# A second DRAM layout for the running sums of log a, and decays of half the first group read from it

## Chip, cores, metric

One NeuronCore of a Trainium2 chip runs the whole program. The metric is the device time of one execution in microseconds; lower is better. Before the change three runs gave 578.08, 579.09 and 579.59 us, a median of 579.09 us.

## What is computed

A decaying linear attention (chunked state-space form) is followed by two mixture-style feed-forward layers. The reference, cut to what matters:

```python
# batch 4, heads 8, seq 768, head_dim 32, d_state 16, chunks of 32
cum = np.cumsum(log_a_chunk, axis=-1)
L = np.exp(cum[..., :, None] - cum[..., None, :]) * causal      # decay from j to i
M = einsum('bhin,bhjn->bhij', Cc, Bc) * L
y = einsum('bhij,bhjd->bhid', M, xc) + einsum('bhin,bhnd->bhid', Cc, state) * exp(cum)[..., None]
state = exp(sum(log_a_chunk)) * state + sum_j Bx * exp(cum_last - cum)
# then, on [3072, 256]:
h = max(x @ w1, x @ w2, x @ w3) @ w_out                         # d_ff 768
z = h @ w_in                                                    # d_ff 2048
out = ((a0 + a1 z + a2 z^2 + a3 z^3) / (1 + |b0||z| + |b1| z^2 + 1e-6)) @ w_out2
```

## The kernel before

The kernel takes chunks of 128 time steps, so that there are six groups (g = 0 to 5) of all four batches, and splits a group into eight units (one batch, four heads). **Stage one** is the attention, some 100 us; **stage two** is the two feed-forward layers, group by group, with fp32 weights split in a high and a low part and three matmuls per product.

Per unit of stage one: `d_mm` (L482) forms the exponent of the decay, cum_i - cum_j below the diagonal and -4096 above, in a PSUM bank `d` on TensorE; ScalarE takes its exponential `e` (L504); `s_mm` (L468) gives the products of C and B, two units at a time; VectorE multiplies the two to `m` (L509); `y_intra` (L511) multiplies `m` with x. Once a group, `state` (L549 to L573) brings the state forward, `y_inter` adds its part, and `prep` (L451) decays C and B by `e0` and `wrev`.

There are two ways to the exponent. In the first group (g = 0) VectorE multiplies the triangle with log a (`tl`, L494) and an fp32 matmul sums that (L490). In the later groups it is one bf16 matmul of two operands in the tiles `lr0` and `lr1`, which serve the groups in turn: constant rows of ones (the input `lrc`) and rows of the running sums, in three bf16 parts that add up to fp32. Those sums are made once: `cum_mm` (L399), split into three parts `cs` on ScalarE and VectorE, one write to DRAM as `cum_d` with the part outermost (L417), and then, for each group from 1 on, `load_cum` (L424) reads them back in seven loads: one for the row operand `rd`, three for `ld`, three for `re`, the operand of the matmul that spreads the decay of C (`sel`, a small matrix of ones copied from lr, L436).

The weights come as 64-bit values in 28 pieces of 512 KB (`plan_conv`, L213): a transfer to one of three raw buffers `wraw` (L241), two passes on ScalarE (L246, L249), three on VectorE (L247, L250, L253), two halves each of two passes on GpSimd (L258, L262), and a copy on ScalarE in between. The names w1, w2, w3 come three times each, then wo (3), win (8), and for stage two wo2 (8).

All transfers are issued by SyncE, in one order. The order on every engine is made ahead by a planner (`Plan.emit`, L91): it takes operations with a cost and a due time and lists them; each engine then runs its list strictly in order. Transfers whose name stands in the list `FIRST` (L37) are due before everything else.

Of the kernel before, what the change touches and what calls it, by code (L numbers as in the profile page):

```python
# [19 lines left out]
CH = 128  # L20
# [10 lines left out]

OL = 6
# [4 lines left out]
FIRST = ["a", "t", "b0", "z0", "n0", "x0", "w1"]  # L37
# [119 lines left out]
def decay_attention_max_moe_rational_moe(  # L157
# [119 lines left out]
    def mark():  # L277
        return _Tile(lambda: None)
# [40 lines left out]
    for nm, bufs in (("pd", 2), ("psc", 4), ("py", 2)):  # L319
# [15 lines left out]
    sel = sp.tile([24, 128], BF16, name="sel")  # L335
# [3 lines left out]
    (act_t, tri_t, trib_t, own_t, la_t, wrev_t, cs_t, sel_t, cum_t, co_t) = (mark() for _ in range(10))  # L339
    rd_t, ld_t, re_t = ([mark() for _ in range(2)], [[mark() for _ in range(3)] for _ in range(2)],  # L340
                        [[mark() for _ in range(3)] for _ in range(2)])
# [75 lines left out]
    load(lambda: cum_d.rearrange("p q r i -> r (p q) i"), cs.rearrange("r p q i -> r (p q) i"), [cum_t], [cs_t], kb=295)  # L417

    for i in (1, 0):
        op("dve", 0.5, lambda i=i: dve.memset(lr[i][64:128].bitcast(F32), 0.0), [], [lr_t[i]])  # L420
        load(lambda i=i: lr[i][0:64], lrc, [lr_t[i]], kb=197, nm=f"l{i}")
    load(lambda: co_raw, coef, [co_t, own_t], kb=68)

    def load_cum(g):  # L424
        q, i, j = g // 3, g % 2, g % 3
        load(lambda: rd[i][0:24], cum_d[:, q].rearrange("p (g u f) i -> p g u (f i)", u=NU, g=3)[:, j],
             [rd_t[i]], [cum_t, lr_t[i]], kb=25)
        for p in range(3):
            load(lambda p=p: ld[i][24 + 4 * p:28 + 4 * p],
                 cum_d[p, q].rearrange("(g u f) j -> g f u j", u=NU, g=3)[j], [ld_t[i][p]], [cum_t, lr_t[i]], kb=16)  # L430
        for p in range(3):
            load(lambda p=p: re[i][8 * p:8 * p + 8].rearrange("h (b i) -> h b i", b=NB),
                 cum_d[p, q].rearrange("(g b h) i -> g h b i", b=NB, g=3)[j], [re_t[i][p]], [cum_t], kb=16)


    op("dve", 0.2, lambda: dve.tensor_copy(  # L436
        out=sel.rearrange("r (q n f) -> r q n f", q=2, f=4),
        in_=ld[1][0:24, :, 0].rearrange("r (q f) -> r q f", q=2)[:, :, None, :].to_broadcast([24, 2, NS, 4])),
       [lr_t[1]], [sel_t])
# [42 lines left out]
    def d_mm(u):  # L482
# [8 lines left out]
        if g == 0:  # L491
# [104 lines left out]
    prep(0)  # L596
    load_cum(1)
# [307 lines left out]
def layout(inputs):  # L905
# [62 lines left out]
```

## Time and profile before

| | |
|---|---|
| median of three runs | 579.09 us |
| the profiled execution, own time | 579.21 us |
| its span (first to last instruction) | 577.3 us |
| TensorE busy | 556.8 us, 96% |
| VectorE, ScalarE, GpSimd busy | 89%, 75%, 76% |
| mean granted TensorE clock | 0.997 |
| read from DRAM, written | 27.27 MB, 5.91 MB |

The profile is one execution. Its page gives the busy share of every engine; the other views used below are the timeline of one engine, the busy time of all engines in chosen windows, the chain of work that ended last, and the instructions of one tensor. PE is TensorE, DVE VectorE, ACT ScalarE, POOL GpSimd, SPq the queue of SyncE that issues transfers. A bracket at the end of a timeline row tells how long the engine stood idle before it and what released it.

### The profile page before, as it was taken

The numbers are of one execution on the slowest core, as the hardware profiler recorded it, in microseconds if no ns is written. First come the engines' busy times: TensorE is split into PE (matmuls) and PEld (weight loads), VectorE is DVE, ScalarE is ACT, GpSimd is POOL, SyncE is SP. The second block draws the span as 40 slices with busy tenths as digits, with TensorE's granted clock in tenths as the row PEclk, the third lists the DMA queues.
The fourth block names the chain that finished last, engine by engine and source line by source line (L and its number), as shares of the span: only waits on it lengthen the run. The fifth ranks groups of instructions, "written<-read, shape, count | busy, mean of one in ns | idle before, by whom it ended". The sixth has DMA issues, their size and how long they took to land.

```text
span 577.3 us, 8164 instructions
## 1 busy us (share of the span) xinstructions
PE 556.8 (96%) x2747; PEld 411.2 (71%) x2758; DVE 511.9 (89%) x777; ACT 435.3 (75%) x756; POOL 440.6 (76%) x410
## 2 busy tenths in 40 slices
PE   8989989989999999999999999999999999999997
PEld 3333433768787788888888888888888888886563
DVE  7888979777999999998889988898898889988996
ACT  4677768556888878878788787778777877778883
POOL 1756767887989967778677877687777997869883
PEclk9999999999999999999999999999999999999999
DMA  6877864533000000101000010000000010000000
GB/s 216 243 270 238 237 233 148 182 110 109 1 1 2 18 20 0 37 1 38 0 1 37 1 33 6 0 20 18 1 1 1 0 37 0 1 1 36 2 0 36
DMA packets 19047, 33.71 MB, mean 58 GB/s; under 512 B 3526, under 2 KB 4030, under 8 KB 19006
## 3 DMA queue, kind: packets, MB, share of 16 engines
q1 hardware_dynamic: 19003, 33.20, 17.9%
q8 instruction: 21, 0.34, 0.2%
q14 instruction: 23, 0.16, 0.1%
HBM read 27.27 MB, written 5.91 MB: 57 GB/s over the span
## 4 chain that ended last, share of the span: by engine, by line
PE 53%; DVE 17%; POOL 17%; issue 4%; ACT 4%; DMA 3%; SPq 2%; POOLq 0%; ACTq 0%; DVEq 0%
PE pg L650 7%; PE pg L652 7%; PE pg L651 6%; PE ph L650 5%; PE ph L652 5%; PE ph L651 5%; PE po L652 4%; PE po L650 4%; PE po L651 4%; POOL glo L853 2%; PE s L477 2%; DMA wraw<-in_w_dram 2%; POOL v L819 2%; POOL hlo L295 2%; DVE pr L845 2%
## 5 line engine op out<-in xcount | busy, mean ns | idle before, releaser
L853 POOL TENSOR_TENSOR glo<-w,ghi 128x512 fp32r<-128x512 f32 x80 | 105.5, 1319 | 16.2 <-ACT ghi L196 16.1
L650 PE MATMUL pg<-xhi,w_hi 128*128 128x512 f32 x202 | 79.1, 392 | 2.8 <-DVE xa L732 2.2
L652 PE MATMUL pg<-xhi,w_lo 128*128 128x512 f32 x202 | 78.8, 390 | 0.0
L651 PE MATMUL pg<-xlo,w_hi 128*128 128x512 f32 x202 | 78.7, 390 | 0.0
L840 ACT ACTIVATE pr<-v,qc 128x512 f32<-128x512 f32 x83 | 57.4, 693 | 22.2 <-DVE v L826 11.3
L295 POOL TENSOR_TENSOR hlo<-xa,hhi 128x512 fp32r<-128x512 f32 x36 | 49.5, 1376 | 26.0 <-ACT hhi L196 25.9
L258 POOL TENSOR_TENSOR wa<-wa,we 128x256 uint32<-128x256 uint32 x56 | 44.2, 800 | 32.9 <-DVE wa L253 32.9
L196 ACT ACTIVATE ghi<-w 128x512 fp32r<-128x512 f32 x80 | 50.4, 630 | 23.9 <-PE po L652 14.2
L650 PE MATMUL ph<-yhi,win_hi 128*128 128x512 f32 x160 | 62.7, 392 | 1.7 <-DVE w L838 1.5
L651 PE MATMUL po<-glo,wo_hi 128*128 128x512 f32 x160 | 62.4, 390 | 0.4 <-POOL glo L853 0.4
L652 PE MATMUL ph<-yhi,win_lo 128*128 128x512 f32 x160 | 62.3, 390 | 0.0
L650 PE MATMUL po<-ghi,wo_hi 128*128 128x512 f32 x160 | 62.3, 390 | 0.0
L652 PE MATMUL po<-ghi,wo_lo 128*128 128x512 f32 x160 | 62.3, 390 | 0.0
L651 PE MATMUL ph<-ylo,win_hi 128*128 128x512 f32 x160 | 62.3, 389 | 0.0
L845 DVE SCALAR_TENSOR_TENSOR pr<-w,co,pr 128x512 f32<-128x512 f32 x83 | 61.9, 746 | 0.0
L819 POOL TENSOR_TENSOR v<-t,v 128x512 f32<-128x512 f32 x44 | 58.1, 1320 | 2.8
L842 DVE SCALAR_TENSOR_TENSOR v<-v,pr 128x512 f32<-128x512 f32 x83 | 56.2, 677 | 2.2 <-ACT pr L841 2.2
L847 DVE SCALAR_TENSOR_TENSOR w<-v,pr 128x512 f32<-128x512 f32 x83 | 56.3, 678 | 0.4
L841 ACT ACTIVATE pr<-pr 128x512 f32<-128x512 f32 x86 | 50.5, 587 | 0.9
L732 DVE TENSOR_TENSOR xa<-xa,pg 128x512 f32<-128x512 f32 x67 | 45.5, 679 | 2.3 <-PE pg L652 2.1
L650 PEld LDWEIGHTS pg<-xhi,w_hi 128*128 128x128 f32 x202 | 37.9, 188 | 12.1 <-DVE xa L732 3.1
L837 POOL TENSOR_TENSOR w<-w,t 128x512 f32<-128x512 f32 x20 | 25.9, 1293 | 24.0 <-DVE v L826 22.1
(167 smaller groups left out, 1485.1 us busy)
## 6 DMA issues: line engine op xcount, KB each, us to landing
wraw<-in_wo_dram SPq DMA_DIRECT2D x11, 512.0 KB
wraw<-in_w_dram SPq DMA_DIRECT2D x9, 512.0 KB
wraw<-in_win_dram SPq DMA_DIRECT2D x8, 512.0 KB
xn<-in_xn_dram SPq DMA_DIRECT2D x6, 512.0 KB
out_dram<-ob SPq DMA_DIRECT2D x12, 256.0 KB
xt_d<-xo SPq DMA_DIRECT2D x10, 256.0 KB
xst<-xt_d SPq DMA_DIRECT2D x10, 256.0 KB
bt<-in_bz_dram SPq DMA_DIRECT2D x6, 256.0 KB
```

What stands on the lines that cost most here:

```text
L196: act.activation(out=o, in_=i, func=AF.Copy)
L295: lambda: e.tensor_tensor(out=lo.t, in0=src(), in1=hi.t.bitcast(F32), op=ALU.subtract),
L650: pe.matmul(dst, wh, hi, start=first, stop=False)
L651: pe.matmul(dst, wh, lo, start=False, stop=False)
L652: pe.matmul(dst, wl, hi, start=False, stop=last)
L819: pop(1.23, lambda: pool.tensor_tensor(out=f(v), in0=f(t1), in1=f(v), op=ALU.mult), [t1], [v])
L840: aop(0.62, lambda: act.activation(out=f(r), in_=f(v), func=AF.Ln, bias=qc), [v], [r])
L841: aop(0.48, lambda: act.activation(out=f(r), in_=f(r), func=AF.Exp, scale=-1.0), [], [r])
L842: dop(0.61, lambda: dve.scalar_tensor_tensor(out=f(v), in0=f(v), scalar=QC, in1=f(r), op0=ALU.add, op1=ALU.mult), [r], [v])
L845: dop(0.61, lambda: dve.scalar_tensor_tensor(out=f(r), in0=f(w), scalar=c(0), in1=f(r), op0=ALU.add, op1=ALU.mult), [w], [r])
L847: dop(0.61, lambda: dve.scalar_tensor_tensor(out=f(w), in0=f(v), scalar=2.0, in1=f(r), op0=ALU.subtract, op1=ALU.mult), [v, r], [w])
L853: pop(1.23, lambda: pool.tensor_tensor(out=f(lo), in0=f(w), in1=f(hi).bitcast(F32), op=ALU.subtract), [w, hi], [lo])
```

## The change

The sums are written to DRAM a second time, as `cup_d`, with the part next to the row, in two writes (one for groups 0 to 2, one for 3 to 5). From this layout one load brings all three parts for `ld` and one all three for `re`, so a group takes three loads. The rows of `lrc` are put in the new order. Group 0 loads its `rd` and `ld` as well (named `r0` in `FIRST`), and its units 4 to 7 take the bf16 way; units 0 to 3 keep `tl`. `lrc` carries the matrix `sel` in 128 more columns, so the copy on VectorE goes; the memsets of `lr` go from VectorE to GpSimd; `lr0` is loaded early (`l0` in `FIRST`).

```diff
+ND = 4
-FIRST = ["a", "t", "b0", "z0", "n0", "x0", "w1"]
+FIRST = ["a", "t", "b0", "z0", "l0", "n0", "x0", "w1", "r0"]
...
     cum_d = dram.tile([3, 2, 96, CH], BF16, name="cum_d")
+    cup_d = dram.tile([2, 96, 3, CH], BF16, name="cup_d")
...
-    lr = [sp.tile([128, NU * CH + T], BF16, name=f"lr{i}") for i in range(2)]
+    lr = [sp.tile([128, NU * CH + T + 128], BF16, name=f"lr{i}") for i in range(2)]
...
-    sel = sp.tile([24, 128], BF16, name="sel")
+    sel = lr[1][0:24, NU * CH + T:]
...
     load(lambda: cum_d.rearrange("p q r i -> r (p q) i"), cs.rearrange("r p q i -> r (p q) i"), [cum_t], [cs_t], kb=295)
-    for i in (1, 0):
-        op("dve", 0.5, lambda i=i: dve.memset(lr[i][64:128].bitcast(F32), 0.0), [], [lr_t[i]])
-        load(lambda i=i: lr[i][0:64], lrc, [lr_t[i]], kb=197, nm=f"l{i}")
+    for q in range(2):
+        load(lambda q=q: cup_d[q], lambda q=q: cs[:, :, q], [cup_t], [cs_t], kb=148)
+    for i in (0, 1):
+        op("pool", 0.9, lambda i=i: pool.memset(lr[i][64:128].bitcast(F32), 0.0), [], [lr_t[i]])
+        load(lambda i=i: lr[i][0:64], lrc, [lr_t[i]], kb=213, nm=f"l{i}")
...
     def load_cum(g):
         q, i, j = g // 3, g % 2, g % 3
+        nm = None if g else "r0"
         load(lambda: rd[i][0:24], cum_d[:, q].rearrange("p (g u f) i -> p g u (f i)", u=NU, g=3)[:, j],
-             [rd_t[i]], [cum_t, lr_t[i]], kb=25)
-        for p in range(3):
-            load(lambda p=p: ld[i][24 + 4 * p:28 + 4 * p],
-                 cum_d[p, q].rearrange("(g u f) j -> g f u j", u=NU, g=3)[j], [ld_t[i][p]], [cum_t, lr_t[i]], kb=16)
-        for p in range(3):
-            load(lambda p=p: re[i][8 * p:8 * p + 8].rearrange("h (b i) -> h b i", b=NB),
-                 cum_d[p, q].rearrange("(g b h) i -> g h b i", b=NB, g=3)[j], [re_t[i][p]], [cum_t], kb=16)
+             [rd_t[i]], [cum_t, lr_t[i]], kb=25, nm=nm)
+        rows = cup_d[q].rearrange("(g r) p i -> g r p i", g=3)[j]
+        load(lambda: ld[i][24:36], rows.rearrange("(u f) p j -> f p u j", u=NU),
+             [ld_t[i]], [cup_t, lr_t[i]], kb=49, nm=nm)
+        if g:
+            load(lambda: re[i].rearrange("r (b i) -> r b i", b=NB), rows.rearrange("(b h) p i -> h p b i", b=NB),
+                 [re_t[i]], [cup_t], kb=49)
...
-    op("dve", 0.2, lambda: dve.tensor_copy(
-        out=sel.rearrange("r (q n f) -> r q n f", q=2, f=4),
...
-        if g == 0:
+        if u < ND:
...
     prep(0)
+    load_cum(0)
     load_cum(1)
...
-            lrc[24 + 4 * p + f, NU * CH + CH * f:NU * CH + CH * f + CH] = -1.0
+            lrc[24 + 3 * f + p, NU * CH + CH * f:NU * CH + CH * f + CH] = -1.0
```

The planner sorts everything anew. Line numbers of the changed kernel are two to six higher. Three places show what that moved.

**SyncE, from the load of the constant rows `lrc` on.** Names: `lr1`, `lr0`, `re1` are the tiles above, `cz1` is C of a group, `wraw_...` a raw weight piece, `DMAHW0` to `DMAHW7` the eight counters on which transfers report in turn. Before:

```order
L283 DMA lr1_126<-in_lrc_dram 64x1536 [waits DMAHW6_49]
L283 DMA bt_232<-in_bz_dram 128x512 [waits DMAHW7_49]
L283 DMA cz1_135<-in_ct_dram 32x512 [waits DMAHW0_49,Pool_49]
L283 DMA re1_128<-cum_d_83 8x4x128 [waits DMAHW3_49,DMAHW1_49]
L283 DMA re1_128<-cum_d_83 8x4x128 [waits DMAHW2_49]
L283 DMA re1_128<-cum_d_83 8x4x128
L241 DMA wraw_255<-in_w1_dram 128x2x512 [waits DMAHW4_49,DVE_49,Activation_49]
L283 DMA cz1_135<-in_ct_dram 32x512 [waits DMAHW5_49]
L283 DMA cz1_135<-in_ct_dram 32x512 [waits DMAHW6_49]
L283 DMA cz1_135<-in_ct_dram 32x512 [waits DMAHW7_49]
L283 DMA xn_284<-in_xn_dram 128x1024 [waits DMAHW0_49]
L283 DMA lr1_126<-cum_d_83 24x1x512 [waits DMAHW1_49]
```

And now, from the second write of `cup_d` (the 19th transfer) to the load of `lr0` from it (the 30th):

```order
L287 DMA cup_d_84<-cs_133 288x1x128 [waits DMAHW2_49]
L287 DMA lr0_126<-cum_d_83 24x1x512 [waits DMAHW5_49,DMAHW3_49]
L287 DMA cz1_135<-in_ct_dram 32x512 [waits DMAHW4_49,Pool_49]
L245 DMA wraw_262<-in_w1_dram 128x2x512 [waits DVE_49,Activation_49]
L287 DMA cz1_135<-in_ct_dram 32x512 [waits DMAHW6_49]
L287 DMA cz1_135<-in_ct_dram 32x512 [waits DMAHW7_49]
L287 DMA cz1_135<-in_ct_dram 32x512 [waits DMAHW0_49]
L287 DMA xn_294<-in_xn_dram 128x1024 [waits DMAHW1_49]
L287 DMA bn_297<-in_bn_dram 128x512 [waits DMAHW2_49]
L287 DMA lr1_127<-cum_d_83 24x1x512 [waits DMAHW3_49]
L245 DMA wraw_304<-in_w2_dram 128x2x512 [waits DMAHW4_49,DVE_49,Activation_49]
L287 DMA lr0_126<-cup_d_84 12x8x128 [waits DMAHW5_49]
```

The first group's sums stand where group 1's stood, behind the second pieces of w1 and w2; the three early loads of `re1` have gone from ahead of the second w1 piece.

**TensorE, around the fifth unit's exponent.** `d_...` are the exponents, `s_...` the products of C and B, `y_...` the outputs. Before, the fifth unit (`d_246`) stood before the first `y`:

```order
L488 LDWEIGHTS trib_124
L488 MATMUL d_246<-trib_124 128x512
L490 MATMUL d_246<-tl_238,tri_s_123 128x512
L520 MATMUL y_262<-m_224,xn_171 32x128 x4
L520 MATMUL y_268<-m_250,xn_171 32x128 x4
```

And now (`d_343`), behind the products of C and B for all eight units and the outputs of the first four:

```order
L479 MATMUL s_266<-cz0_134,bt_143 128x512
L479 MATMUL s_267<-cz0_134,bt_143 128x512
L522 MATMUL y_240<-m_264,xn_172 32x128 x4
L522 MATMUL y_257<-m_274,xn_172 32x128 x4
L479 MATMUL s_290<-cz0_134,bt_143 128x512
L479 MATMUL s_291<-cz0_134,bt_143 128x512
L490 LDWEIGHTS trib_125
L490 MATMUL d_343<-trib_125 128x512
L492 LDWEIGHTS lr0_126
L492 MATMUL d_343<-lr0_126 128x512
```

Between the last `s` and the first row on `lr0` only the constant part of the exponent stands.

**VectorE, up to the fifth unit's product** (`m_367` before, `m_360` now; the rows on `wa` are weight conversions, three to a piece). Before:

```order
L494 TENSOR_TENSOR tl_306<-tri_s_123,la_130 128x512
L253 SCALAR_TENSOR_TENSOR wa_257<-wraw_214,wa_257 128x512
L509 TENSOR_TENSOR m_330<-s_229,e_252 128x512
L247 TENSOR_SCALAR wa_314<-wa_314 128x512
L566 TENSOR_TENSOR st_344<-d_319,co_raw_84 128x512
L250 TENSOR_SCALAR wa_314<-wa_314 128x512
L436 COPY sel_133<-lr1_126 24x128
L253 SCALAR_TENSOR_TENSOR wa_314<-wraw_220,wa_314 128x512
L509 TENSOR_TENSOR m_367<-s_290,e_297 128x512
```

And now:

```order
L511 TENSOR_TENSOR m_274<-s_250,e_246 128x512
L251 TENSOR_SCALAR wa_271<-wa_271 128x512
L254 TENSOR_SCALAR wa_271<-wa_271 128x512
L257 SCALAR_TENSOR_TENSOR wa_271<-wraw_221,wa_271 128x512
L251 TENSOR_SCALAR wa_312<-wa_312 128x512
L254 TENSOR_SCALAR wa_312<-wa_312 128x512
L257 SCALAR_TENSOR_TENSOR wa_312<-wraw_225,wa_312 128x512
L464 TENSOR_TENSOR bn_297<-bn_297,wrev_132 128x512
L251 TENSOR_SCALAR wa_331<-wa_331 128x512
L254 TENSOR_SCALAR wa_331<-wa_331 128x512
L257 SCALAR_TENSOR_TENSOR wa_331<-wraw_262,wa_331 128x512
L511 TENSOR_TENSOR m_360<-s_266,e_353 128x512
```

Four pieces of weights are converted before the fifth product where three were, and the second `bn` is decayed before it.

## Rows read from the trace of the kernel before

**Rows 1.** The page, part 1: busy us (share) and instructions of each engine.

```profile
PE 556.8 (96%) x2747; PEld 411.2 (71%) x2758; DVE 511.9 (89%) x777; ACT 435.3 (75%) x756; POOL 440.6 (76%) x410
```

**Rows 2.** Windows: length, busy us by engine, granted clock (PEclk), DMA share, GB/s.

```profile
14.30:23.40 9.10, 9.10 (x69) 3.70 (x67) 9.10 (x17) 6.94 (x12) 6.22 (x8) 1.00 0.84 244
23.40:32.40 9.00, 6.64 (x52) 2.12 (x51) 5.67 (x9) 5.71 (x11) 5.25 (x6) 1.00 0.94 269
...
60.00:100.00 40.00, 34.67 (x341) 14.69 (x345) 35.54 (x61) 30.03 (x54) 28.36 (x37) 1.00 0.65 206
100.00:126.00 26.00, 23.20 (x105) 18.16 (x106) 20.44 (x26) 15.25 (x28) 22.50 (x26) 1.00 0.43 145
126.00:131.00 5.00, 5.00 (x16) 3.92 (x16) 3.02 (x6) 2.89 (x6) 2.89 (x3) 0.66 0.28 105
131.00:570.00 439.00, 436.46 (x1873) 349.94 (x1872) 399.69 (x593) 346.00 (x597) 353.22 (x304) 1.00 0.04 14
```

**Rows 3.** Timeline, TensorE: start, us, line, out<-in; fifth unit's matmul, first one on lr.

```profile
14.49 1.02 PE L490 MATMUL d<-tl,tri_s 128*128 128x512 f32 x2
...
24.12 0.38 PE L490 MATMUL d<-lr 128*128 128x512 bf16 x1
```

**Rows 4.** Timeline, VectorE, three windows; in brackets the idle time before and its releaser.

```profile
14.84 2.06 DVE L494 TENSOR_TENSOR tl<-tri_s,la 128x512 f32<-128x512 f32 x2
...
22.69 2.47 DVE L509 TENSOR_TENSOR m<-s,e 128x512 f32<-128x512 f32 x4
...
30.70 0.69 DVE L462 TENSOR_TENSOR bn<-bn,wrev 128x512 f32<-128x512 f32 x1 [3.33 <-DMA bn<-in_bn_dram]
...
81.25 0.43 DVE L247 TENSOR_SCALAR wa<-wa 128x512 f32<-128x512 f32 x1 [3.23 <-ACT wa L246]
...
99.27 0.68 DVE L509 TENSOR_TENSOR m<-s,e 128x512 f32<-128x512 f32 x1
```

**Rows 5.** Timeline, GpSimd, 0 to 40 us.

```profile
0.73 1.84 POOL L368 MEMSET cz<- 128x1024 f32 x2 [0.29 <-POOLq L953]
...
14.47 1.88 POOL L258 TENSOR_TENSOR wa<-wa,we 128x256 uint32<-128x256 uint32 x2 [11.90 <-DVE wa L253]
```

**Rows 6.** One tensor's instructions, cum_d: issue in ns, minimum/median/maximum.

```profile
L283 SPq DMA_DIRECT2D lr<-cum_d x20: 286/393/817, 19.7 to 69.2; - x20
```

**Rows 7.** Timeline, SyncE's queue, 0 to 60 us: start and length of each issue.

```profile
9.85 0.34 SPq L283 DMA_DIRECT2D cum_d<-cs  x1
...
13.30 1.15 SPq L283 DMA_DIRECT2D re<-cum_d  x3
...
14.81 0.40 SPq L241 DMA_DIRECT2D wraw<-in_w_dram  x1
...
19.70 2.00 SPq L283 DMA_DIRECT2D lr<-cum_d  x4
...
22.69 0.38 SPq L241 DMA_DIRECT2D wraw<-in_w_dram  x1
```

**Rows 8.** The chain that ended last, 0 to 130 us: weight pieces under way (start, us).

```profile
5.70 5.33 DMA wraw<-in_w_dram
...
22.69 6.27 DMA wraw<-in_w_dram
...
73.72 6.16 DMA wraw<-in_win_dram
```

**Rows 9.** Timeline, ScalarE, 0 to 40 us.

```profile
28.98 0.66 ACT L249 ACTIVATE we<-wraw 128x512 uint32<-128x512 uint32 x1 [2.71 <-DMA wraw<-in_w_dram]
...
29.55 1.07 ACT L504 ACTIVATE e<-d 128x512 f32<-128x512 f32 x2
```

**Rows 10.** Timeline, TensorE, 123 to 136 us.

```profile
125.80 0.50 PE L650 MATMUL pg<-xhi,w_hi 128*128 128x512 f32 x1 [1.94 <-DVE xa L732]
...
127.82 0.63 PE L651 MATMUL ph<-xlo,w_hi 128*128 128x512 f32 x1
128.24 0.63 PE L652 MATMUL ph<-xhi,w_lo 128*128 128x512 f32 x1
```

More of the change, by code (lines that the diff above doesn't have):

```diff
@@ L323, in decay_attention_max_moe_rational_moe @@
     trib = sp.tile([128, 2, 128], BF16, name="trib")
-    lr = [sp.tile([128, NU * CH + T], BF16, name=f"lr{i}") for i in range(2)]
+    lr = [sp.tile([128, NU * CH + T + 128], BF16, name=f"lr{i}") for i in range(2)]
     ld = [t[:, 0:NU * CH].rearrange("p (u j) -> p u j", u=NU) for t in lr]
-    rd = [t[:, NU * CH:] for t in lr]
+    rd = [t[:, NU * CH:NU * CH + T] for t in lr]
     re = [sp.tile([24, T], BF16, name=f"re{i}") for i in range(2)]
@@ L334, in decay_attention_max_moe_rational_moe @@
     cs = sp.tile([96, 3, 2, CH], BF16, name="cs")
-    sel = sp.tile([24, 128], BF16, name="sel")
+    sel = lr[1][0:24, NU * CH + T:]
     cz = [sp.tile([128, 4, T], F32, name=f"cz{i}") for i in range(2)]
     cz_t, lr_t = [[mark() for _ in range(4)] for _ in range(2)], [mark() for _ in range(2)]
-    (act_t, tri_t, trib_t, own_t, la_t, wrev_t, cs_t, sel_t, cum_t, co_t) = (mark() for _ in range(10))
-    rd_t, ld_t, re_t = ([mark() for _ in range(2)], [[mark() for _ in range(3)] for _ in range(2)],
-                        [[mark() for _ in range(3)] for _ in range(2)])
+    (act_t, tri_t, trib_t, own_t, la_t, wrev_t, cs_t, cum_t, cup_t, co_t) = (mark() for _ in range(10))
+    rd_t, ld_t, re_t = ([mark() for _ in range(2)] for _ in range(3))
     xg, bg, ctg, btg = {}, {}, {}, {}
@@ L425, in load_cum @@
         q, i, j = g // 3, g % 2, g % 3
+        nm = None if g else "r0"
         load(lambda: rd[i][0:24], cum_d[:, q].rearrange("p (g u f) i -> p g u (f i)", u=NU, g=3)[:, j],
-             [rd_t[i]], [cum_t, lr_t[i]], kb=25)
-        for p in range(3):
-            load(lambda p=p: ld[i][24 + 4 * p:28 + 4 * p],
-                 cum_d[p, q].rearrange("(g u f) j -> g f u j", u=NU, g=3)[j], [ld_t[i][p]], [cum_t, lr_t[i]], kb=16)
-        for p in range(3):
-            load(lambda p=p: re[i][8 * p:8 * p + 8].rearrange("h (b i) -> h b i", b=NB),
-                 cum_d[p, q].rearrange("(g b h) i -> g h b i", b=NB, g=3)[j], [re_t[i][p]], [cum_t], kb=16)
-    op("dve", 0.2, lambda: dve.tensor_copy(
-        out=sel.rearrange("r (q n f) -> r q n f", q=2, f=4),
-        in_=ld[1][0:24, :, 0].rearrange("r (q f) -> r q f", q=2)[:, :, None, :].to_broadcast([24, 2, NS, 4])),
-       [lr_t[1]], [sel_t])
+             [rd_t[i]], [cum_t, lr_t[i]], kb=25, nm=nm)
[5 more added lines that the diff above has]
+                 [re_t[i]], [cup_t], kb=49)
     op("act", 0.2, lambda: act.activation(out=co[:, 4:6], in_=co_raw[:, 4:6], func=AF.Abs), [co_t], [co_t])
@@ L455, in prep @@
             op("pe", 0.22, lambda: pe.matmul(p0.t, sel, re[g % 2], start=True, stop=True),
-               [sel_t, *re_t[g % 2]], [p0], when["p0", g])
+               [lr_t[1], re_t[g % 2]], [p0], when["p0", g])
             e0[g] = new("s2", "e0", 2)
@@ L501, in d_mm @@
             op("pe", 0.46, lambda: mm(lambda: ld[g % 2][:, k], lambda: rd[g % 2]),
-               [trib_t, lr_t[g % 2], rd_t[g % 2], *ld_t[g % 2]], [t], when["d", u])
+               [trib_t, lr_t[g % 2], rd_t[g % 2], ld_t[g % 2]], [t], when["d", u])
         e_t[u] = e = new("s4", "e", 4)
@@ L931, in layout @@
     d["tri"] = tri.astype(np.float32)
-    lrc = np.zeros((64, NU * CH + T), np.float32)
+    lrc = np.zeros((64, NU * CH + T + 128), np.float32)
     for p in range(3):
+        for h in range(NH):
+            lrc[3 * h + p, NU * CH + T + 64 * (h // 4) + h % 4:NU * CH + T + 64 * (h // 4) + 64:4] = 1.0
         for u in range(NU):
```

## The prediction

> **What bounds the kernel now.** The page first: TensorE is busy for nearly the whole span [rows 1]. The windows by stage then show where it isn't [rows 2]: from 131 to 570 us it has 436.46 of 439 us, so stage two has no room in it, and only its start can move. The room lies in stage one, up to about 100 us, and in the first group of stage two up to 131 us: TensorE stands for 2.4 us in 23.4 to 32.4 us, for 5.3 in 60 to 100, for 2.8 in 100 to 126, and runs at a lower clock from 126 to 131. In 60 to 100 us VectorE has 35.54 of 40 us, as much as TensorE, so in stage one VectorE's order sets the pace as often as TensorE's. The DMA share is 0.84 and 0.94 in the two stretches from 14.3 to 32.4 us: there the transfers queue up, and a small one waits behind big ones. That queue is what this change gets into.
>
> **TensorE and VectorE work removed.** For units 4 to 7 of the first group the fp32 matmul on tl, 1.02 us, becomes a bf16 one on lr, 0.38 us [rows 3]: 4 x 0.64 = 2.6 us less on TensorE. VectorE loses four products tl (two took 2.06 us [rows 4]), 4.1 us, the two memsets of lr and the copy to sel. Both savings lie before the point where, below, both engines stand and wait for a load, so I cost them at nothing; what they free is used or lost in that wait. The memsets go to GpSimd, which made two larger ones in 1.84 us and then stood for 11.90 us [rows 5]: two of 0.1 to 0.92 us fit in there, cost nothing.
>
> **SyncE's queue.** A group's sums came in seven loads and now in three: 35 loads in all become 17 (five groups by three, and two for the first group), against two more writes. Loads to lr took 0.39 us in the median [rows 6], so SyncE spends some 16 x 0.39 = 6 us less on issuing. It is on the path only where a weight piece stands behind such loads. I take 1.0 us for this, between nothing and the 3.2 us that VectorE waited at 81.25 us [rows 4] behind a weight piece that was 6.16 us under way [rows 8].
>
> **The new wait.** The fifth unit's matmul started at 14.49 us, on data made on the chip [rows 3]. Now it needs the first group's sums from DRAM. SyncE issues in order, and the order shown above has the load of lr0 from cup_d as the 30th transfer, behind two weight pieces, xn, bn and four pieces of cz, and since the program counts landings on eight counters in turn, each transfer waits for the eighth before it to land: for this one that is the second w1 piece (the 22nd). In the trace the write of the sums goes out at 9.85 us, the second w1 piece at 14.81 [rows 7]. Weight pieces landed 5.33 and 6.27 us after their issue in this queue [rows 8], so the second w1 piece lands between 20.1 and 21.1 us, some 0.5 us later for the lrc load that now goes ahead of it (213 KB take 0.9 us at 244 GB/s [rows 2], but some of the early queue is free), and another 1.0 us for the two writes to cup_d. Those two writes are bounded thus: cum_d's, of 576 pieces of 256 bytes, went out at 9.85 us and was read from 13.30 us without a wait in between [rows 7], so at most 3.45 us for both halves together and at least the 0.6 us that 147 KB take at 244 GB/s [rows 2]; I take 0.5 us for each of the two. The load of lr0 therefore goes out at about 22 us. It lands, at best, as the four loads of lr did whose issue ended at 21.70 us and whose matmul ran at 24.12 [rows 3, 7], 2.4 us later: 24.4 us. At worst it waits like a weight piece, 6.27 us: 28.3 us. The second w2 piece is right ahead of it in the same queue, as then, so I take the upper half, 27 us.
>
> There is a second lock on the same door. On ScalarE the exponential for that unit now stands behind the conversion of the second w2 piece. Before, that conversion waited 2.71 us for its piece and began at 28.98 us [rows 9]; the piece had been issued at 22.69 us [rows 7], and is now issued about a microsecond sooner, which makes some 27 us again. Conversion 0.66 us and exponential, half of 1.07 us [rows 9], make 28.2 us by this lock, and 27 + 0.38 + 0.53 = 27.9 by the other: the fifth product m starts at about 28.0 us, where it started at 22.69 [rows 4]. **Stage one is late by 5.3 us there**, between 3.5 and 7.5.
>
> A rule of the Trainium skill speaks against the two extra writes: by "DMA: Bandwidth & Descriptors", Specifications, transfers under 512 bytes miss line rate because they are read, modified and written. The trace bounds the same thing at 3.45 us for 576 such pieces, and by that upper end the two writes would cost 2.4 us more than I take, and the sum would end at 580.6 us instead of 578.2.
>
> **What is paid back.** From that fifth product to the last one of stage one (99.27 us [rows 4]) VectorE has the same 44 products to make, one product bn less (0.69 us), and one weight piece was converted in the wait, while one more has to be converted before the end: these two cancel. So 0.7 us less work. Before, this stretch held a wait of 3.33 us for the third bn [rows 4], whose load stood in the crowded queue. Now the second bn is made during the wait, and the third is asked for only after VectorE has gone through the late products, by when the queue has drained: I take the whole 3.3 us as gone, with nothing as the other end. The queue saving above gives 1.0 us (0 to 3.2).
>
> Then the start of stage two. TensorE stood for 2.8 us in 100 to 126 us [rows 2], 1.94 of them at 125.80 us behind a maximum that VectorE made late because of the weight conversions between them [rows 10]. After that wait the granted clock was 0.66 in the mean of 126 to 131 us [rows 2], the lower of the two levels (1.2 GHz) for part of it: matmuls 0.42 us apart [rows 10] against 0.23 at full clock (the mean of 436.46 us over 1873 matmuls [rows 2]). With 34% of 5 us missing the clock cost 1.7 us. So 4.5 us are to be had here. In the new order one piece more has been converted when stage two begins, and GpSimd, busy for 22.50 of 26 us there [rows 2], has less left. I take 2.0 of the 4.5 us; nothing and all are the ends.
>
> And the clock in stage one: TensorE stands longer than those 1.94 us before lr0 lands, so it may come back at the lower level and lose up to the same 1.7 us, at a place where VectorE sets the pace: 0.7 us.
>
> **The sum,** against the profiled execution's 579.21 us (span 577.3 and 1.9 around it; 0.1 above the median of the three runs, 579.09): + 5.3 (late) - 0.7 (work) - 3.3 (bn) - 1.0 (queue) - 2.0 (start of stage two) + 0.7 (clock) = - 1.0, so **578.2 us**. All low ends together: 3.5 - 0.7 - 3.3 - 3.2 - 4.5 = - 8.2; all high ends: 7.5 - 0.7 + 1.7 = + 8.5. Stage two's own order is sorted anew, too; with 2.5 us of standing in 439 I cost that at nothing.
>
> **Rivals.** *The wait is not paid back* (slower). One mechanism: SyncE's load of lr0 stands behind the weight pieces, TensorE's weight load for the fifth unit waits, the clock falls, and the pieces that VectorE wants later still arrive when they did. Then + 5.3 - 0.7 + 1.7 - 2.0 = + 4.3, 583.5 us. For it: a DMA share of 0.94 with 2.4 us of standing in the same stretch [rows 2]; against it, that bn's wait came from that very stretch. It decides from about 3.5 us on: a start of the fifth product after 28 us with the bn wait still there.
>
> *The conversions' lead pays more* (faster). The wait is filled with four weight conversions in a row; if the pieces stay ahead, the waits at 81.25 us and at 125.80 us both go: + 5.3 - 0.7 - 3.3 - 3.2 - 4.0 + 0.7 = - 5.2, 574.0 us. For it: after 60 us both waits are for weight pieces [rows 4, 10]; against it, VectorE's 35.54 of 40 us leave little to gain.
>
> *The fewer loads change nothing,* since SyncE mostly waits for landings and for raw buffers, and the lead in weights doesn't last to stage two; only bn's wait is paid back: + 5.3 - 0.7 - 3.3 = + 1.3, 580.5 us, no change by the bound below.
>
> **How the numbers follow.** 0.3%, or 1.7 us, is about what a measurement of this kernel tells from no change. Forecast 578.2 us: 0.40; its own range 576 to 580.9 gives faster 0.13, same 0.25, slower 0.02. Not paid back, 583.5 us: 0.26, all slower. Lead pays more, 574.0 us: 0.28, all faster. Only bn's wait paid back, 580.5 us: 0.06, same. So faster 0.41, same 0.31, slower 0.28. The range 573.0 to 584.5 us reaches over the middles of both outer cases and leaves out about a tenth on either side.
>
> **What would show it.** In the changed kernel's trace: the first matmul on lr between 26 and 28 us, with TensorE standing before it for 6 us or more and its wait put down to a load of lr or to the exponential behind the w2 piece; the granted clock below 1.00 somewhere in 20 to 32 us; no wait of VectorE for bn; stage two's first matmul between 99 and 104 us; fewer than 4.5 us lost between there and 131 us. I am wrong if the first matmul on lr runs before 24 us (then faster than forecast), or if the stretch from it to stage two is not shorter than before (then the first rival).

## The result, and the profile after

The changed kernel is **slower: 585.11 us** in the median of six executions (583.12 to 586.67) against 578.74 us; the ratio is 1.0103, with an interval of 1.0082 to 1.0124. The forecast was 578.2 us, its range 573.0 to 584.5. The profiled execution, the slowest of the six, took 586.67 us, with a span of 584.9 us and a mean granted clock of 0.985.

The windows of [rows 2] in the changed kernel (columns as there):

```profile
14.30:23.40 9.10, 3.72 (x33) 1.17 (x33) 6.72 (x13) 6.04 (x11) 4.73 (x7) 0.93 0.98 303
23.40:32.40 9.00, 4.84 (x30) 2.45 (x31) 6.29 (x9) 4.98 (x9) 7.35 (x10) 0.50 0.87 264
...
131.00:570.00 439.00, 435.10 (x1869) 350.45 (x1868) 395.30 (x583) 345.29 (x590) 351.53 (x300) 1.00 0.04 14
```

Between 14.3 and 23.4 us TensorE has 3.72 us of work where it had 9.10, and then runs at 0.50, its 1.2 GHz level, for 9 us. Stage two is about as full as before (435.10 of 439 us, 436.46 before), so the loss lies ahead of it. TensorE's timeline of the changed kernel:

```profile
27.26 0.59 PE L492 MATMUL d<-lr 128*128 128x512 bf16 x1 [7.78 <-POOL wa L262]
...
29.51 1.98 PE L557 MATMUL d<-xn,bn 128*64 128x128 f32 x16
...
69.43 0.43 PE L522 MATMUL y<-m,xn 128*32 128x128 f32 x8 [2.66 <-DVE m L511]
...
108.66 0.50 PE L653 MATMUL pg<-xhi,w_hi 128*128 128x512 f32 x1
...
133.23 0.50 PE L653 MATMUL pg<-xhi,w_hi 128*128 128x512 f32 x1 [1.93 <-DVE xa L735]
```

The first of these rows is the fifth unit's matmul, the second the state matmul of the first group, the third a stall that h2 takes up, the fourth the start of stage two, the last a wait behind that start. The first bracket names a conversion on GpSimd; g1, which moves only the load of lr0, has this matmul at 20.94 us, so it is the load that counts. Before, stage two started here (TensorE, before):

```profile
100.36 0.50 PE L650 MATMUL pg<-xhi,w_hi 128*128 128x512 f32 x1
```

So stage two starts 8.30 us late; the span is 7.6 us longer, so 0.7 us comes back behind that. VectorE's timeline in the changed kernel, to be held against [rows 4]:

```profile
28.56 1.50 DVE L511 TENSOR_TENSOR m<-s,e 128x512 f32<-128x512 f32 x2 [0.73 <-ACT e L506]
...
31.54 0.69 DVE L568 TENSOR_TENSOR st<-d,co_raw 128x512 f32<-128x512 f32 x1 [1.48 <-PE d L557]
...
36.14 1.27 DVE L464 TENSOR_TENSOR bn<-bn,wrev 128x512 f32<-128x512 f32 x1 [1.19 <-DMA bn<-in_bn_dram]
...
67.10 1.67 DVE L464 TENSOR_TENSOR bn<-bn,wrev 128x512 f32<-128x512 f32 x1 [1.37 <-DMA bn<-in_bn_dram]
```

The fifth product starts 5.87 us late (28.56 against 22.69 us [rows 4]). From there to stage two it takes 80.1 us where it took 77.7: another 2.4 us are lost, nothing is paid back. (By the medians the whole loss is 6.4 us, so a middling execution loses less than this one, the slowest.) What VectorE's waits behind that product are put down to (us in total, times, longest), in the changed kernel, then before:

```profile
DVE d L568 <- PE d L557: 2.6, 3, 1.5
DVE bn L464 <- DMA bn<-in_bn_dram: 2.6, 2, 1.4
DVE m L511 <- PE s L479: 2.1, 4, 1.2
DVE m L511 <- ACT e L506: 1.7, 4, 0.9
DVE wa L251 <- ACT wa L250: 1.7, 4, 1.1
DVE st L568 <- PE d L557: 1.5, 1, 1.5
```

```profile
DVE wa L247 <- ACT wa L246: 3.5, 2, 3.2
DVE bn L462 <- DMA bn<-in_bn_dram: 3.3, 1, 3.3
DVE m L509 <- PE s L477: 1.8, 2, 1.2
DVE d L566 <- PE d L555: 0.4, 1, 0.4
```

The waits for weight conversions fell by 1.8 us and those for bn by 0.8 (3.33 less 2.56). But VectorE now waits 4.1 us for TensorE's state products, where it waited 0.4, and 1.7 us for exponentials, where it had no such wait. TensorE is busy for 72.85 us in this stretch, against 68.61 before: late products of the first group now lie in it, and its granted clock was 0.95 in the mean against 1.00. How much each of the two makes, no run separates.

For bn VectorE still waits, now twice. SyncE's queue in the changed kernel tells why:

```profile
22.10 0.39 SPq L245 DMA_DIRECT2D wraw<-in_w_dram  x1
22.54 0.43 SPq L287 DMA_DIRECT2D lr<-cup_d  x1
...
29.80 0.38 SPq L245 DMA_DIRECT2D wraw<-in_w_dram  x1
31.53 0.33 SPq L287 DMA_DIRECT2D bn<-in_bn_dram  x1
...
62.10 0.79 SPq L287 DMA_DIRECT2D lr<-cum_d  x1
63.80 0.34 SPq L287 DMA_DIRECT2D bn<-in_bn_dram  x1
```

and the third bn's issue before:

```profile
24.88 0.53 SPq L283 DMA_DIRECT2D bn<-in_bn_dram  x1
```

bn has two buffers. The third load needs the one that the first group's state matmul (L557) reads, and that stands on TensorE behind the late matmuls on lr. The load goes out 6.65 us later than before. Most of that is its place in the new order, since the row ahead of it ended at 30.18 us only; the other 1.35 us SyncE stood until the state matmul was done. The fifth load stands behind the loads of lr0 for a later group.

### The profile page after: what moved, and what is told of

It is laid out like the page before. It is cut to its first block, busy times and chain, and to the rows that moved or that the text cites. A ratio compares the mean times of both kernels' runs of the same rounds, so it can differ in the third digit from the quotient of the medians.

```text
span 584.9 us, 8133 instructions
## 1 busy us (share of the span) xinstructions
PE 556.8 (95%) x2742; PEld 409.9 (70%) x2754; DVE 508.1 (87%) x770; ACT 437.2 (75%) x756; POOL 442.0 (76%) x412
## 4 chain that ended last, share of the span: by engine, by line
PE 54%; POOL 18%; DVE 16%; ACT 4%; issue 4%; DMA 4%; SPq 0%; POOLq 0%; DVEq 0%; ACTq 0%
PE pg L653 7%; PE pg L655 7%; PE pg L654 7%; PE ph L653 5%; PE ph L654 5%; PE ph L655 5%; PE po L655 4%; PE po L654 4%; PE po L653 4%; POOL glo L856 3%; PE s L479 2%; DMA wraw<-in_w_dram 2%; POOL v L822 2%; POOL hlo L299 2%; DVE pr L848 1%
```

## The experiments

Theory A: the wait for the first group's sums is the loss. Theory B: the new layout and its writes are. Theory C: the new sorting of stage one is. The planner sorts everything anew when an operation changes, so the first kernels below are sorted by it, and later ones have an order written out by hand.

### Sorted by the planner

**e1_all_tl**, the layout alone:

```diff
-ND = 4
+ND = 8
-FIRST = ["a", "t", "b0", "z0", "l0", "n0", "x0", "w1", "r0"]
+FIRST = ["a", "t", "b0", "z0", "n0", "x0", "w1"]
...
-    load_cum(0)
```

> The second layout with its three loads a group stays, but all eight units of the first group take their decays from tl again, as before the change, and nothing is read for the first group. Theory A (the whole loss is the wait for the first group's sums): the wait is gone, stage two starts at 99 to 101.5 us again, the time is 0.993 to 1.002 of before (575 to 580 us). Theory B (the two extra writes and the new layout crowd the early queue): still 1.005 to 1.01, 582 to 585 us. Theory C (any new sorting of stage one loses some us against an order that happened to be good): 1.004 to 1.012.

Measured: 580.76 us, 1.0027 (1.0010 to 1.0044). None of the three: the early wait is gone, and a stall stands in its place, at the matmul that reads the second group's re (TensorE; the load that the bracket names is another):

```profile
31.63 0.58 PE L457 MATMUL d<-re,lr 24*128 24x512 bf16 x1 [4.12 <-DMA cz<-in_ct_dram]
```

**e7_two_marks_all_tl** takes that away: as e1, and the plan counts cup_d's halves apart.

```diff
...
-        load(lambda q=q: cup_d[q], lambda q=q: cs[:, :, q], [cup_t], [cs_t], kb=148)
+        load(lambda q=q: cup_d[q], lambda q=q: cs[:, :, q], [cup_t[q]], [cs_t], kb=148)
...
```

> The new layout alone in the planner's own order (tl for all of the first group), with the two halves of cup_d as two things in the plan, so that the load of re for the second group goes out ahead of the second half's write. If e1's loss against f1 (4.0 us) is the stall of 4.12 us for that load at 27 to 31 us: no such stall, 0.995 to 1.000 of before. If the new sorting costs in another place: 1.001 to 1.005.

Measured: 580.58 us, 1.0022 (1.0008 to 1.0037). That wait fell to 1.27 us and the time stayed: so that stall was not e1's price; what took its place the run doesn't say.

**e2_two_marks** is the changed kernel with the same two marks, so that the planner itself puts the load of lr0 early.

> The changed kernel, but the two halves of the second layout count as two things in the plan: the second half's write no longer waits for the first half's, and the first group's load waits for the first half alone. The load of lr0 comes right behind the write, ahead of the second w1 piece, instead of the 30th. Theory A: first matmul on lr at 18 to 22 us instead of 27.3, time 0.995 to 1.003 of before (576 to 581 us). Theory B: one of the extra writes moves late, so half of the loss stays: 1.003 to 1.006. Theory C: 1.004 to 1.012.

Measured: 584.14 us, 1.0080 (1.0056 to 1.0104). The matmul came at 20.62 us and the fifth product at 21.75, as theory A asked, and the time hardly fell: by the intervals it is not to be told from the changed kernel's. Theory A in its simple form is wrong for the planner's orders.

**e4_old_layout** takes the last four units of the first group from the sums, without the second layout; its edit of the kernel before (ND is 4):

```diff
...
-        if g == 0:
+        if u < ND:
...
+    load_cum(0)
     load_cum(1)
```

> The kernel before with the first group's units 4 to 7 taken from the sums, in the old layout: four loads for the first group (no re), no second layout, seven loads for the others. The loads for lr0 stand ahead of the second w1 piece here, since they wait for one write alone. Theory A: first matmul on lr at 19 to 22 us, the fifth product no later than 23.5 us, time 0.995 to 1.003 of before. Theory B: no extra writes, so 0.99 to 1.002. Theory C: 1.004 to 1.012 in spite of the early load.

Measured: 583.56 us, 1.0073 (1.0053 to 1.0094), with the fifth product at 21.36 us. It loses without a second layout or a second write, so theory B isn't needed for a loss; theory C held so far.

**e3_warm** keeps TensorE busy in the wait:

```diff
         def mm(w, x):
+            if u == ND:
+                for _ in range(32):
+                    pe.matmul(t.t, zero[:, 0:CH], zero, start=True, stop=True)
```

> The changed kernel with 32 matmuls on zeros (some 7 us) put ahead of the fifth unit's first matmul, where TensorE stands for 7.8 us; the order of all else is meant to stay. If the clock after the wait is part of the loss: granted clock near 1.00 in 23 to 35 us, stage two 1 to 3 us earlier, time 1.005 to 1.008 of before (582 to 584 us). If VectorE alone sets the pace behind the wait (theory A in its pure form, a shift by the late load): 1.009 to 1.012 as the changed kernel.

Measured: 587.48 us, 1.0143 (1.0122 to 1.0164). A window of e3_warm:

```profile
20.00:25.00 5.00, 5.00 (x25) 2.29 (x24) 1.95 (x3) 2.24 (x4) 4.26 (x6) 1.00 0.70 243
```

The clock stayed up in these 5 us and nothing was gained. But the planner sorted this anew as well, and the fifth product came at 29.77 us, later than without, so it settles little on the clock; f6 asks again.

### The order of before, written out by hand

Here each engine runs the list of the kernel before, with only the named rows different. **f1_layout** has the new layout alone in that order; its edit of the changed kernel, with e1's change of FIRST and the list of numbers left out:

```diff
-ND = 4
+ND = 8
+ORDER = [
...
+        order = ORDER
...
-    load_cum(0)
```

> The order of every engine is the one of the kernel before, written out by hand; only the layout is the changed kernel's: two writes to cup_d (the first right behind cum_d's, the second behind the second w2 piece), three loads in the place of seven, memsets on GpSimd, no copy to sel. The first group has tl for all eight units. Theory C (the loss is the new sorting of stage one): 0.996 to 1.001 of before, 576.5 to 579.5 us. Theory B (the writes and the layout cost): 1.002 to 1.006. Theory A has no wait here: 0.996 to 1.001.

Measured: 576.77 us, **0.9956** (0.9941 to 0.9972): faster than before. Theory B is refuted; e1 and e7, the same work as sorted by the planner, are 3.8 to 4.1 us behind it. VectorE's third bn, for which it waited 3.33 us before [rows 4], and stage two's start in f1:

```profile
28.77 0.72 DVE L468 TENSOR_TENSOR bn<-bn,wrev 128x512 f32<-128x512 f32 x1 [1.11 <-DMA bn<-in_bn_dram]
```

```profile
98.74 0.50 PE L656 MATMUL pg<-xhi,w_hi 128*128 128x512 f32 x1
```

**f2_early** adds the first group's second half from the sums:

> As f1, and the first group's units 4 to 7 take their decays from the sums: lrc for lr0 goes out behind the first w1 piece, the two loads of lr0 ahead of the second w1 piece. Every other instruction stands where it stood before. First matmul on lr at 18 to 21 us, the fifth product at 21 to 23 us. Theory C: 0.994 to 1.001 of before (575 to 579.5 us), since the 4 us that VectorE saves are worth something between nothing and all. If taking the decays from the sums costs in itself, without a new sorting and without a wait: 1.003 to 1.008, as in the run with the old layout (1.0073).

Measured: 581.71 us, 1.0051 (1.0032 to 1.0069). TensorE takes the fifth unit at 14.8 us in this order and stands (first row TensorE of f2, then VectorE):

```profile
19.46 0.58 PE L496 MATMUL d<-lr 128*128 128x512 bf16 x1 [4.30 <-DMA lr<-cup_d]
```

```profile
26.41 0.69 DVE L572 TENSOR_TENSOR st<-d,co_raw 128x512 f32<-128x512 f32 x1 [2.74 <-PE d L561]
...
28.22 2.48 DVE L515 TENSOR_TENSOR m<-s,e 128x512 f32<-128x512 f32 x4
```

The matmul ran when it was expected, but the fifth product, expected at 21 to 23 us, starts in the last of these rows at 28.22: in this order the first group's state stands ahead of it on VectorE.

**f3_late** was to move the load back, but its matmuls of units 4 to 6 stand ahead of the load in the written order and didn't wait for it: the load goes out at 24.70 us, and they ran without the sums of their columns.

> As f2, but the load of lr0 from cup_d stands behind the second w2 piece, where the changed kernel has it. First matmul on lr at 26 to 28 us, fifth product at 27 to 29 us. Theory A (the wait is the loss and isn't paid back): 4 to 7 us over f2, 1.006 to 1.012 of before. Theory C (the new sorting is the loss, and a wait of 5 us in the stretch where VectorE also waits for weights is largely paid back): 0 to 2.5 us over f2.

Measured: 581.55 us, 1.0041 (1.0022 to 1.0061). It tells nothing on the late load (its first matmul on lr ran at 18.86 us); f9 asks again.

**f5_late_units** is f2 with units 4 to 7 taken later. TensorE's rows, in short:

```diff
-d4 y0 y1 d5 s4,5 y2 d6 state y3 d7 s6,7
+y0 y1 s4,5 y2 y3 s6,7 d4 d5 d6 state d7
```

> As f2 (the order of before, the first group's second half from the sums, its loads ahead of the second w1 piece), but TensorE, ScalarE and VectorE take units 4 to 7 later: TensorE has the products s and y of the first four units and s of the last four ahead of them, and VectorE the conversion of the w3 piece. If f2's loss (2.9 us against before, 4.9 against f1) is that TensorE stands at the fifth unit's matmul until the sums are back at 19.5 us: no wait over 3 us there, 0.992 to 0.999 of before. If the sums cost in themselves (lrc for lr0 and the two loads push the weights back): 1.002 to 1.006.

Measured: 578.78 us, 1.0001 (0.9987 to 1.0014). The whole work of the changed kernel, and no loss: so what that kernel loses by 1.0103 comes from where its rows stand. Against f1 it is 2.6 us behind all the same (1.0001 less 0.9956), although VectorE has four products tl less to make (4.0 us in f1). By the pages its busy time is no shorter for it, 510.2 us against 510.5. What the 2.6 us are stays open.

**f9_late_load** is f5 with one row moved on SyncE's queue:

```diff
-lr0<-cup_d
 wraw<-in_w1 (second piece)
...
 wraw<-in_w2 (second piece)
+lr0<-cup_d
```

> As f5 (the changed kernel's work in the old order, 1.0001 of before), with one row moved: the load of lr0 from cup_d goes behind the second w2 piece on SyncE's queue, where the changed kernel has it, and the matmuls wait for it. First matmul on lr at 26 to 28 us instead of 22.4, the fifth product at 27 to 29 us instead of 23.73. If the wait isn't paid back (the prediction's first rival): 3.5 to 5.5 us over f5, 1.006 to 1.010 of before. If it is largely paid back behind it: 0 to 2 us over f5, 1.000 to 1.004.

Measured: 585.05 us, **1.0117** (1.0087 to 1.0148), 6.7 us over f5 by the ratios (4.8 to 8.6 by the intervals). The middle lies above the 3.5 to 5.5 expected of a wait that isn't paid back; the intervals reach into that. That one row costs as much as the whole change. TensorE in f5, then in f9:

```profile
22.43 0.63 PE L496 MATMUL d<-lr 128*128 128x512 bf16 x1
...
100.56 0.50 PE L657 MATMUL pg<-xhi,w_hi 128*128 128x512 f32 x1
```

```profile
27.02 0.59 PE L496 MATMUL d<-lr 128*128 128x512 bf16 x1 [4.19 <-DMA lr<-cup_d]
...
106.03 0.50 PE L657 MATMUL pg<-xhi,w_hi 128*128 128x512 f32 x1
```

The matmul is 4.59 us later, stage two 5.47. VectorE's fifth product and fifth bn in f5, then in f9:

```profile
23.73 0.69 DVE L515 TENSOR_TENSOR m<-s,e 128x512 f32<-128x512 f32 x1 [0.98 <-ACT e L510]
...
61.08 1.13 DVE L468 TENSOR_TENSOR bn<-bn,wrev 128x512 f32<-128x512 f32 x1
```

```profile
28.27 0.69 DVE L515 TENSOR_TENSOR m<-s,e 128x512 f32<-128x512 f32 x1 [5.25 <-ACT e L510]
...
64.84 1.14 DVE L468 TENSOR_TENSOR bn<-bn,wrev 128x512 f32<-128x512 f32 x1
```

SyncE's queue in f9, what it waited for between its two rows (us in total, times, longest), and the window from 25 us in f9, then in f5:

```profile
23.53 0.56 SPq L291 DMA_DIRECT2D re<-cup_d  x1
30.77 0.36 SPq L291 DMA_DIRECT2D bn<-in_bn_dram  x1
```

```profile
SPq L291 <- PE d L561: 6.6, 1, 6.6
```

```profile
25.00:30.00 5.00, 2.98 (x13) 1.31 (x15) 1.38 (x2) 2.10 (x4) 0.18 (x1) 0.50 0.29 91
```

```profile
25.00:30.00 5.00, 3.84 (x40) 1.81 (x37) 3.40 (x5) 3.42 (x8) 1.28 (x1) 0.96 1.02 333
```

The late load acts like this: the state matmul comes late, the third bn's buffer comes free late, SyncE stands 6.6 us at its row, and the transfers behind it don't run: a DMA share of 0.29 against 1.02, 91 GB/s against 333. That this standing is what keeps the wait from being paid back is argued, not tested. The rows of VectorE show how late it is: 4.54 us at the fifth product, 3.76 at the fifth bn, 5.47 at stage two. Some 0.8 us is paid back at first, and then nothing: VectorE is busy for 49.40 of the 53 us from 32 to 85 us, and no wait for bn is there to fall away, in f5 or in f9. The last 1.7 us are lost between 85 us and stage two, where the granted clock was 0.92 in the mean from 85 to 106 us and 1.00 in f5; whether the clock makes them, no run shows.

**f6_warm** and **f7_bn_later** ask what else is to be had. f6 is f5 with 13 matmuls on zeros in two gaps of TensorE and the third bn's product later; f7 is f1 with that product later.

> As f5, with 5 and 8 matmuls on zeros where TensorE stood for 0.97 and 1.64 us at 16.4 and 17.8 us, and the product of the third bn behind the twelfth unit's. If the lower clock at 20 to 26 us is what f5 still loses against f1: granted clock near 1.00 there, fifth product at 21.5 to 23 us, 0.995 to 0.999 of before. If transfers set the pace there: 0.999 to 1.002, as f5.

Measured: 578.88 us, 0.9988 (0.9969 to 1.0007). Its window shows the clock held where f5 had 0.50:

```profile
20.00:25.00 5.00, 4.55 (x37) 1.96 (x36) 4.01 (x6) 3.37 (x7) 3.63 (x6) 1.00 0.87 292
```

Over f5 the ratios give it 0.8 us, by the intervals anything from a loss of 0.6 to a gain of 2.1; the third bn's row is moved in it as well.

> As f1 (the fastest so far, 0.9956), with VectorE's product of the third bn moved behind that of the twelfth unit, so that nothing stands behind its load. If the wait of 1.11 us for it is on the path: 0.992 to 0.995. If VectorE's work behind it only waits for something else: 0.995 to 0.997.

Measured: 576.25 us, **0.9943** (0.9924 to 0.9963), the fastest here, and not to be told from f1 by the intervals. It beats both kernels: the new layout without the first group's sums, in the old order.

**f8_double** is f1 with two more writes in pieces of 256 bytes:

```diff
+    more_d = dram.tile([2, 96, 3, CH], BF16, name="more_d")
...
+    more = [(lambda q=q: nc.sync.dma_start(out=more_d[q], in_=cs[:, :, q])) for q in range(2)]
...
```

> As f1, with two more writes of the same size and pieces (288 pieces of 256 bytes each) to a tensor that nobody reads, right behind the first half of cup_d. By the prediction's 0.5 us a write: 0 to 1.0 us over f1, 0.9956 to 0.998 of before. By the upper end of its bound (1.7 us a write, which is what the rule on transfers under 512 bytes would give): 3 us over f1, 1.000 to 1.002.

Measured: 577.93 us, 0.9978 (0.9963 to 0.9992): 0.0022 over f1, so 1.3 us for the two, 0.6 us each; by the two intervals between nothing and some 1.2 us each. Nobody reads what they write.

### Rows moved in the changed kernel's own order

**g1_load_early** moves one row, the load of lr0 from cup_d, ahead of the second w1 piece.

> The changed kernel's own order on every engine, with one row moved: the load of lr0 from cup_d goes out right behind that from cum_d, ahead of the second w1 piece. First matmul on lr at 19 to 21 us instead of 27.3. If the second lock holds (the fifth unit's exponential stands behind the conversion of the second w2 piece on ScalarE), the fifth product still comes at 27 to 28.5 us and the time stays at 1.007 to 1.0105 of before; if the load was the only lock, the fifth product comes at 21 to 23 us and the time falls to 1.000 to 1.004.

Measured: 585.07 us, 1.0094 (1.0073 to 1.0115). TensorE and ScalarE in g1:

```profile
20.94 0.38 PE L496 MATMUL d<-lr 128*128 128x512 bf16 x1 [1.88 <-POOL wa L266]
```

```profile
28.06 0.66 ACT L257 ACTIVATE we<-wraw 128x512 uint32<-128x512 uint32 x1 [1.70 <-DMA wraw<-in_w_dram]
28.62 1.07 ACT L510 ACTIVATE e<-d 128x512 f32<-128x512 f32 x2
```

The matmul ran 6.3 us sooner, its exponential waited behind the conversion of the w2 piece, and the fifth product came at 29.24 us: the second lock of the prediction is there, and holds alone.

**h1_unlocked** moved those exponentials and products ahead as well.

> The changed kernel's order with both locks opened: the load of lr0 from cup_d goes out early as in the run before, and on ScalarE and VectorE the exponentials and products of units 4 to 6 stand ahead of the conversions of the second w1 and w2 pieces. All else in the changed kernel's order. The fifth product should come at 21.5 to 23.5 us instead of 28.56. If the early wait is the loss and isn't paid back: stage two 4 to 6 us earlier than 108.66, time 1.000 to 1.004 of before. If something later in the order sets the end of stage one (the stall at 65 to 70 us): stage two 0 to 3 us earlier, 1.006 to 1.010.

Measured: 586.67 us, 1.0121 (1.0090 to 1.0152). It missed both cases: the fifth product came at 26.14 us only, since the second bn's product stood ahead of it and waited 1.96 us, and the third bn then waited 3.05 us, at 38.73.

**h2_bn_first** moves the fifth bn's load ahead of the loads of lr0 at 60.27 us.

> The changed kernel's order with one row moved on SyncE's queue: the fifth load of bn (issued at 63.80 us) goes ahead of the two loads of lr0 and the weight piece between them (60.27 to 62.10 us). If the stall of TensorE at 66.6 to 69.4 us and the lower clock behind it come from that load: the stall shrinks to under 1.5 us, the clock stays at 1.00 in 70 to 75 us, stage two 2 to 4 us earlier, 1.004 to 1.008 of before. If VectorE's order sets the stall anyway: 1.009 to 1.011.

Measured: 583.94 us, 1.0085 (1.0060 to 1.0111), by the intervals not to be told from the changed kernel. In the profiled execution, the fastest of six, stage two starts 3.5 us sooner, at 105.19 us. TensorE's stall, and the window behind it, in h2 (the changed kernel had 0.67 there):

```profile
67.58 0.43 PE L526 MATMUL y<-m,xn 128*32 128x128 f32 x8 [0.75 <-DVE m L515]
```

```profile
70.00:75.00 5.00, 4.85 (x71) 2.90 (x70) 3.78 (x8) 4.33 (x8) 3.28 (x5) 1.00 0.76 268
```

**h3_both_bn** also moves the third bn's product behind the twelfth unit's.

> The changed kernel's order with two rows moved: the fifth load of bn ahead of lr0's loads on SyncE (as h2, 1.0085), and VectorE's product of the third bn behind that of the twelfth unit. If the third bn is on the path as it was in f7 (0.8 us there): 0.5 to 1.5 us under h2, 1.006 to 1.0075 of before. If not: 1.008 to 1.009.

Measured: 582.13 us, 1.0063 (1.0039 to 1.0087). The two bn rows together are worth 0.0040 of the changed kernel's 0.0103, some 2.3 us, by the intervals 0.5 to 4.2.

**k1_rows_moved** moves all named rows at once.

> The changed kernel's order with these rows moved at once: on SyncE the load of lr0 from cup_d right behind that from cum_d, the third bn ahead of the next bt, the fifth bn ahead of lr0's loads; on ScalarE the exponentials of units 4 to 8 ahead of the conversions of the second w2 piece and of the w3 piece behind it; on VectorE the products of units 4 to 7 ahead of the second w1 piece's conversion and the product of the third bn behind that of the twelfth unit. If these rows are the loss: ninth product at 30 to 34 us instead of 37.67, stage two at 100 to 103 us, 0.999 to 1.004 of before. If the loss is spread over the whole order: 1.006 or more.

Measured: 588.34 us, 1.0159 (1.0133 to 1.0184). The ninth product came at 33.41 us as expected, but the exponentials put ahead held the weight conversions back (VectorE, then SyncE, in k1):

```profile
41.14 0.69 DVE L515 TENSOR_TENSOR m<-s,e 128x512 f32<-128x512 f32 x1 [3.45 <-ACT e L510]
```

```profile
33.06 0.39 SPq L291 DMA_DIRECT2D re<-cup_d  x1
42.49 0.40 SPq L249 DMA_DIRECT2D wraw<-in_w_dram  x1
```

SyncE issued nothing for 9 us. Moving rows by name opens a new hole; this run doesn't say which rows of the new order lose its 6 us.

## Why the prediction was wrong

*The new wait* was right in place and nearly in size: first matmul on lr at 27.26 us (27 forecast), fifth product at 28.56 (28.0), 5.9 us late (5.3). Both locks are real: f9 has the late load alone, g1 the late exponential alone.

*Work removed, costed at nothing:* right. f5 has four products tl less on VectorE than f1 and is slower.

*The two writes at 0.5 us each:* 0.6 by f8. By the Trainium skill, "DMA: Bandwidth & Descriptors", Specifications, pieces under 512 bytes miss line rate; the upper end that the prediction worked out for it, 1.7 us a write, is excluded.

*What is paid back* is **the step that failed.** Between the fifth product and stage two the sum took 5.0 us back (0.7 for work, 3.3 for bn, 1.0 for the queue); the profiled execution lost 2.4 us more there. The queue's part came: VectorE waits 1.8 us less for weight conversions. The bn part came to 0.8 us of 3.3 (3.33 less 2.56). The prediction took the third bn's wait as gone, "asked for only after VectorE has gone through the late products, by when the queue has drained". It is asked for late, but behind other rows, and its buffer hangs on the state matmul behind the late ones: VectorE waits 1.19 us at 36.14 us, and 1.37 at 67.10 for the fifth. And a term is missing: the late chain makes new waits, 4.1 us for the state products and 1.7 us for exponentials, where 0.4 us stood before. f9 shows by one row that such a delay isn't paid back: 4.6 us late at the matmul are 5.5 at stage two and 6.7 in the time, without any wait for bn. Where nothing came late, the bn wait did fall with the shorter queue (f1: 1.11 us, and the whole layout gains 2.5 us there, where 1.0 was taken for the queue).

*The start of stage two, 2.0 us:* 0.7 us came, all that is made good behind that start. TensorE waits 1.93 us for the maximum at 133.23 us, as it waited 1.94 us at 125.80 [rows 10], and f1 and f7, whose stage two starts at 98.74 and 96.11 us, have 1.93 too. One piece more was in hand, as the prediction counted, and doesn't touch that wait.

*The clock, 0.7 us:* it fell for longer than taken (0.50 over 9 us). What that costs isn't settled. f6 held it up where nothing came late, for 0.8 us or nothing; e3's order changed with it. But the changed kernel's executions go from 583.12 us at a mean clock of 0.991 to 586.67 at 0.985, f9's have 0.985 to 0.990 and f5's 0.988 to 0.997: late work and a lower clock come together here, and part of the new waits may be the clock's: the state matmul that VectorE waits for took 1.98 us at 29.51 us, at 0.50, and 1.09 us before, at 19.79 us and 1.00.

So **the first rival was the right one**: "the wait is not paid back", 583.5 us, with the signs it named: the fifth product after 28 us and the bn wait still there. It had a chance of 0.26 and was 1.6 us short of the median, since it saw no further loss behind the wait and still took 2.0 us back at the start of stage two. Of its mechanism the late load and the fallen clock are there; that the weight pieces still arrive when they did isn't what shows: the waits for weights fell, and those on TensorE and ScalarE rose.

Not foreseen was how much the sorting matters. In the old order the steps add up: layout - 2.5 us, sums of the first group + 2.6, late load + 6.7, together + 6.8, beside the + 6.0 of the change. In the planner's orders the layout alone costs 1.3 to 1.6 us (e7, e1), and an early fifth product saves little (e2, e4: 21.75 and 21.36 us, and losses of 0.0080 and 0.0073). So in the changed kernel's own order the late load is one cause among others: opening both locks (h1, the fifth product 2.4 us sooner) gained nothing, the two rows of bn some 2.3 us (h3). Which rows lose the rest stays open.

## What to carry to other kernels

Before data that is made on the chip is replaced by the same data read back from DRAM, count the way there and back in a loaded queue, and what runs in order behind the first reader; a saved 4 us on an engine that then waits is worth nothing. A delay is paid back only out of waits that stand behind it and fall away with it: list them in the new order, ask for each whether it hangs on the late work itself (a buffer that delayed matmuls read, a product behind them in the queue), and expect a dense stretch to keep what it is given (f9: 3.8 us late at the fifth bn, with VectorE busy for 49.40 of 53 us). And where a planner sorts anew, test the edit in the old order, too; here the layout is 2.5 us faster there and 1.3 to 1.6 us slower in the planner's.

## What the runs showed that was not expected

The way through DRAM was about 9 us in this queue: in f2 the write goes out at 10.32 us and the matmul that reads it starts at 19.46, while tl had the same unit at 14.49 us [rows 3].

SyncE standing for one buffer left the DMA engines mostly idle in f9: a share of 0.29 and 91 GB/s, where f5 moves 333 GB/s in the same stretch. The Trainium skill, "DMA: Bandwidth & Descriptors", Anatomy of one DMA — SWDGE (gpsimd) path, says that DMA engines do not wait on semaphores and that the wait happens on the issuing sequencer; its section is on GpSimd's transfers, and this trace agrees for SyncE's, with 6.6 us of standing on SyncE.

Executions of one kernel differ by as much as the smaller steps here: the twelve of f5 went from 577.51 to 581.15 us, the slowest at the lowest mean clock (0.988), but 577.51 us came at 0.996 and 579.59 at 0.997, so the clock is not all of it. A difference of 0.3% between two single executions is within that spread.
